# Inverses in 16-row blocks, a routing table by matrix products and a written-out order in a chunked recurrence with an expert layer

## The chip, the cores and the metric

The kernel runs on one core of a Trainium2 chip. The metric is device time in microseconds (us), the median of the runs shown. A core has the matrix engine TensorE (PE; its weight loads, PEld, overlap its products), VectorE (DVE), ScalarE (ACT), GpSimd (POOL) and the queues that issue transfers (SP above all here). Each engine takes its instructions in the order in which the program lists them. TensorE's clock is granted at one of two levels, 1.2 or 2.4 GHz; the profile prints 0.5 for the lower and 1.0 for the higher.

## The reference

Two parts, one after the other. The first is a recurrence over 768 steps for 4 batches and 8 heads with a 40x40 state:

```python
for t in range(S):
    y[:, :, t] = np.einsum('bhd,bhde->bhe', rt, state)
    Sa = np.einsum('bhde,bhe->bhd', state, at)
    state_decay = state * wt[:, :, None, :] - np.einsum('bhd,bhe->bhde', Sa, bt)
    state = state_decay + np.einsum('bhd,bhe->bhde', vt, kt)
```

Its output, as 3072 rows of 320, goes to a layer of 8 experts with one expert per row:

```python
expert_idx = np.argmax(x @ w_gate, axis=1)
...
if counts[e] < capacity:
    disp[e, counts[e]] = x[i]
...
h = np.maximum(np.einsum('ecd,edf->ecf', disp, w1), 0.0)
y = np.einsum('ecf,efd->ecd', h, w2)
...
out[i] = gate_w[i] * y[expert_idx[i], pos[i]]
```

## The kernel before, in words

**The scan.** The 768 steps are cut into 6 blocks (`i`) of 128, each of two chunks of 64 (`c`); batches go in two pairs (`pr`). For each block and pair `prep` loads w, a, k|b and r and multiplies them by running products of w (two scans of 1032 elements on VectorE). `unit` forms for each chunk the triangular 64x64 matrices of all 16 (batch, head): `nn` (evacuated to `ns`), `kk` (masked to `tm`) and the turned k|b (`bk`). `inverse` inverts the triangles of a whole block at once: the 32x32 diagonal blocks are transposed so that each partition holds one block (L562), are eliminated column by column in place (`elim`, L474 to L479), are transposed back (L486, L491), and `comb` joins the two 32-blocks of each 64 by two products. Block 0 alone (`SIX = (0,)`) eliminates 16x16 blocks and joins them first to 32 by products of 32 rows (`join`). `chain` then carries the state: `zz`, `sa` (a product with the inverse, written into `vu` beside v), `uT` (transposes of `vu`), `mT` (scores M, masked into `vu[:, 0]`), `yy` (outputs and new state in one accumulation, moving 128 columns per head), `turn` (the state turned). `gate` turns the outputs of a block to rows (x) and forms the logits with x as the stationary operand and `w_gate` moving. `route` picks the expert, counts places and scatters (expert slot, row, gate weight) to a table `meta` in DRAM, four indirect transfers per block.

**The experts.** For each expert the weights are loaded, scaled and split into two float16 parts (L1092, L1093), the rows of `meta` are loaded, turned to indices on POOL (L1126 to L1128), the rows of x are gathered by indirect transfers (L1131) and transposed by DMA (L1265), then come the products `hidden` (L1280), the ReLU and split (L1285, L1288), the products `result` (L1154) and the scatter of the output rows (L1160). Experts 0 and 1 take their first 384 rows from blocks 0 to 4 only, so they can begin before the last block is routed.

**The order.** Steps are put into named threads with their engines and buffers; a planner (`Schedule.order`) with costs, priorities (`LATER`) and choices between engines ("A...|V...") decides one order for all engines, and the program is emitted in it. PSUM has three double tiles `pp` and two single tiles `p1`; a step that takes one waits until its last reader is done.

## Time and profile before

| | us |
|---|---|
| runs shown | 667.86, 673.58, 674.64 |
| median | 673.58 |
| the profiled execution | 677.24 |
| its span (first to last instruction) | 675.5 |
| its mean granted clock | 0.874 |

The profiled execution is 3.7 us above the median. Its span leaves out 1.7 us before the first and after the last instruction. Busy times of an engine are unions of its instructions, so an engine that is busy 90% of a stretch may still be waiting in the other tenth for a result of another one. A product's record holds its way through the array; the distance from one start to the next tells what a stream costs.

### The profile page before, as it was taken

How to read it: one execution, taken by the hardware profiler on the slowest of the kernel's cores; microseconds unless marked ns; L12 is line 12 of the kernel's file. 1: busy time of each engine (PE TensorE's matmuls, PEld its weight loads, DVE VectorE, ACT ScalarE, POOL GpSimd, SP SyncE). 2: the span in 40 equal slices, each digit the busy share in tenths (PEclk: the TensorE clock that was granted, in tenths of full speed). 3: DMA queues.
4: the chain of work that ended last, by engine and by line, in shares of the span. 5: the costliest groups of instructions: out<-in, count | busy, mean ns of one | idle time of the engine just before them, and what ended most of it. 6: DMA issues, size and time to landing. Idle time of an engine off the chain costs nothing.

```text
span 675.5 us, 25339 instructions
## 1 busy us (share of the span) xinstructions
PE 551.9 (82%) x11268; PEld 428.6 (63%) x11268; DVE 437.5 (65%) x844; ACT 289.6 (43%) x567; POOL 154.7 (23%) x231
## 2 busy tenths in 40 slices
PE   1626989799588788899779789696997999999993
PEld 1525877688487678788768777553674455555462
DVE  6986788989896789799949825344443544545310
ACT  9513643644364245445623451233442545534320
POOL 6210010212023000310112022422243342352112
PEclk9665898999758696999879857967998999999998
DMA  6761044123502251235110231674739868957101
GB/s 177 202 168 35 4 113 142 59 78 108 147 30 21 73 143 48 57 80 150 45 34 15 61 113 33 115 209 125 208 87 207 232 158 255 245 125 199 38 11 43
DMA packets 71447, 74.19 MB, mean 110 GB/s; under 512 B 36399, under 2 KB 60177, under 8 KB 70368
## 3 DMA queue, kind: packets, MB, share of 16 engines
q1 hardware_dynamic: 67168, 62.79, 35.7%
q0 software_dynamic: 4160, 9.69, 4.9%
q8 instruction: 90, 1.47, 1.0%
q14 instruction: 29, 0.24, 0.1%
HBM read 57.17 MB, written 10.40 MB: 100 GB/s over the span
## 4 chain that ended last, share of the span: by engine, by line
issue 32%; PE 32%; DVE 17%; POOL 8%; DMA 4%; ACT 4%; SPq 1%; POOLq 1%; another core or an unknown queue 0%; DVEq 0%; ACTq 0%
PE pp L268 19%; PE p L268 7%; POOL out_dram L1160 4%; DVE tmp L477 4%; DVE nu L479 3%; PE pp L649 2%; POOL a L1131 2%; DMA px<-in_w_dram 2%; DVE vu L318 1%; DVE kb L371 1%; DVE xu L486 1%; POOL vT L1131 1%; DVE gx L351 1%; DVE px L360 1%; ACT ns L54 1%
## 5 line engine op out<-in xcount | busy, mean ns | idle before, releaser
L314 POOL TENSOR_SCALAR_AFFINE_SELECT tm<-tm 64x512 f32<-64x512 f32 x42 | 31.3, 746 | 163.7 <-ACT tm L312 148.6
L479 DVE TENSOR_TENSOR nu<-nu,tmp 128x87 f32<-128x87 f32 (+12 forms) x164 | 59.8, 365 | 5.6
L1160 POOL DMA_INDIRECT out_dram<-tm,ri x32 | 32.4, 1012 | 135.3 <-ACT tm L1315 104.0
L477 DVE TENSOR_TENSOR tmp<-xu,nu 128x87 f32<-128x87 f32 (+12 forms) x164 | 59.3, 361 | 4.2
L268 PE MATMUL pp<-vu,bk 128*40 128x128 f32 (+1 forms) x768 | 52.7, 295 | 6.3 <-DVE vu L318 4.7
L268 PEld LDWEIGHTS pp<-vu,bk 128*40 128x40 f32 x768 | 44.5, 129 | 11.4 <-DVE vu L318 5.4
L1280 PE MATMUL pp<-xT,kb 128*128 128x448 f16 (+5 forms) x256 | 47.2, 319 | 0.0
L268 PE MATMUL p<-nu,ns 64*32 64x32 f32 (+1 forms) x1024 | 23.6, 217 | 26.3 <-DVE nu L491 23.5
L50 POOL COPY x<-x 128x128 f16<-128x128 f16 x18 | 13.2, 734 | 137.6 <-ACT x L50 51.6
L268 PE MATMUL pp<-rv,vT 64*64 64x64 f32 x1536 | 34.0, 228 | 12.2 <-issue 8.3
L268 PE MATMUL pp<-a,kb 64*64 64x64 f32 x768 | 23.4, 274 | 22.8 <-DVE kb L371 20.4
L318 DVE TENSOR_TENSOR vu<-pp,mask 128x1024 f32<-128x1024 f32 x24 | 29.1, 1218 | 18.4 <-PE pp L268 16.8
L436 ACT ACTIVATE bk<-pp,sgn 128x320 f32<-128x320 f32 x48 | 22.6, 525 | 39.9 <-PE pp L268 26.5
L268 PEld LDWEIGHTS pp<-rv,vT 64*64 64x64 f32 x1536 | 28.8, 139 | 17.1 <-issue 11.5
L268 PEld LDWEIGHTS p<-nu,ns 64*32 64x32 f32 (+1 forms) x1024 | 21.8, 138 | 27.3 <-DVE nu L491 22.7
L1285 ACT ACTIVATE nt<-pp 128x448 f16<-128x448 f32 (+2 forms) x40 | 16.9, 476 | 48.9 <-PE pp L1280 43.7
L268 PE MATMUL p<-a,kb 64*64 64x64 f32 x768 | 32.6, 242 | 3.2 <-DVE nu L479 1.4
L268 PEld LDWEIGHTS pp<-a,kb 64*64 64x64 f32 x768 | 19.8, 180 | 24.2 <-issue 15.7
L1288 DVE SCALAR_TENSOR_TENSOR px<-pp,nt 128x448 f16<-128x448 f32 (+2 forms) x20 | 10.0, 539 | 38.2 <-ACT nt L1285 30.2
L1018 POOL DMA_INDIRECT meta<-mt,sloti x24 | 24.0, 1000 | 46.4 <-DVE mt L1015 33.4
L1280 PE MATMUL pp<-xT,px 128*128 128x448 f16 (+2 forms) x128 | 33.6, 322 | 0.2 <-DVE rv L1288 0.2
L268 PEld LDWEIGHTS p<-a,kb 64*64 64x64 f32 x768 | 29.9, 156 | 4.0 <-issue 1.5
(220 smaller groups left out, 1375.9 us busy)
## 6 DMA issues: line engine op xcount, KB each, us to landing
vu<-in_moe_w_dram SPq DMA_DIRECT2D x32, 320.0 KB
kb<-in_kb_dram SPq DMA_DIRECT2D x24, 320.0 KB
px<-in_w_dram SPq DMA_DIRECT2D x12, 512.0 KB
vu<-in_vt_dram SPq DMA_DIRECT2D x48, 128.0 KB
px<-in_moe_w_dram SPq DMA_DIRECT2D x12, 512.0 KB
xd<-x SPq DMA_DIRECT2D x24, 192.0 KB
a<-in_a_dram SPq DMA_DIRECT2D x24, 160.0 KB
rv<-in_rv_dram SPq DMA_DIRECT2D x24, 160.0 KB
```

The costliest lines, as they stand in the source:

```text
L268: TT.matmul(out, l, r, start=start, stop=True, skip_group_check=True)
L314: G.affine_select(out[half(x)], out[half(x)], pattern=[[0, n] for n in sh[1:-1]] + [[1, C]], compare_op=ALU.is_gt, fill=0.0, base=0, chann ...
L318: V.tensor_mul(out, in_, m.to_broadcast(sh))
L436: A.activation(U["bk"][:, x].rearrange("p h d -> p (h d)"), U["pi"][:, x, 0:HD], AF.Copy, scale=sgn[:, x:x + 1])
L477: V.tensor_mul(tv, xu[:, :, s + 1:ne, s:s + 1].to_broadcast([P, nb, n, m]), nu[:, :, s:s + 1, 0:m].to_broadcast([P, nb, n, m]))
L479: V.tensor_add(nu[:, :, s + 1:ne, 0:m], nu[:, :, s + 1:ne, 0:m], tv)
L649: TT.transpose(p[:, x, k * P:k * P + P], U["vu"][:, 1, x, k].rearrange("p r d -> p (r d)"), ident)
L1018: nc.gpsimd.indirect_dma_start(out=meta_v[t][:, :], out_offset=bass.IndirectOffsetOnAxis(ap=su[:, t:t + 1], axis=0), in_=mt[:, t, :], in_o ...
L1131: nc.gpsimd.indirect_dma_start(out=xt(j)[:c].rearrange("p a c -> p (a c)"), out_offset=None, in_=src[:, :], in_offset=bass.IndirectOffsetO ...
L1160: nc.gpsimd.indirect_dma_start(out=out_v[used[0] % (8 * E)][:, :], out_offset=bass.IndirectOffsetOnAxis(ap=ri.bitcast(U32)[:c, j, 1:2], ax ...
L1280: nc.tensor.matmul(s_["h", f + z][:, :n], l, rr, start=m % 7 == 0 and m < 14, stop=m >= 14)
L1285: nc.scalar.activation(s_["H"](0, f), s_["h", f][:, :n], AF.Relu)
```

## The change

- **Inverses.** All six blocks are eliminated as 16x16 blocks (14 steps with two blocks per partition instead of 30 steps). A step of 84 or more elements per partition is cut into two halves of rows, the second in a thread `inverse_b`. The join of 16 to 32 is done by products of 64 rows: `split` (two scaled copies with a mask of the 32-halves) lays the blocks out in `yq`, then 32 products into 64x32, `split` again, 32 products into 48x16, and a masked add on VectorE.
- **M and SA|v in one row.** `vu` holds M | SA|v | M in one row of 256, so `yy` moves 104 columns per head and not 128. v comes a second time, transposed, from DRAM (`load_x`, 24 transfers of 256 KB); `uT` transposes 64x64 blocks of SA alone, half as much to evacuate. The output of `yy` is taken in two instructions, not one.
- **Slot table by products.** Instead of `meta` in DRAM each block forms two one-hot matrices on VectorE (`hot_p`, 512 elements, `hot_j`, 3 x 192), multiplies them (4 products of 96 columns, `tabled`), and adds the result to a table in SBUF (`fold`); `index` turns the table to row indices and weights. The 24 scatters, the loads of `meta` and POOL's index instructions are gone.
- **Logits** with `w_gate` stationary: 8 products of 128 columns into four groups of 16 rows, a copy, and a product that adds the four groups.
- **139 unread products** (`warm`): float16, 128 stationary and 512 moving columns, written to the PSUM tile that the next step takes, before that step; nothing reads them. The list puts them in 88 places, all ahead of the last block's routing.
- **New order.** The planner is not used; the order is a list of step names in the text (`ORDER`), `/1` for the second choice of engine, `~n` for n unread products, and every load goes to SP.

```diff
+ORDER = """
+load_w load_kb decay0*2 decay_k0 inverse_0 load_a decay0 nn0*2 load_w load_kb decay1*2 unit decay_k1 load_v kk0
...
+    def warm(self, n, take):
+        for _ in range(n):
+            x = self.bufs[next(y for y in take if y in ("pp", "p1"))][0]
+            x = x if len(x.shape) == 2 else x[:, 0]
+            self.nc.tensor.matmul(x, self.spare[:, 0:P], self.spare[:, None, :].to_broadcast([P, 2, 2 * P]), start=True,
+                                  stop=True, skip_group_check=True)
...
-    SIX = (0,)
+    SIX = (0,1,2,3,4,5,)
...
+            rows = [(s + 1, ne)]
+            if nb * (ne - 1 - s) * m >= 84:
+                h = s + 1 + (ne - s) // 2
+                rows = [(s + 1, h), (h, ne)]
...
+        def split(y, x):
+            for z in range(2):
+                scale(two(y, z), x(z).rearrange("p (u x) t -> p u x t", x=2), mlo[:, z:z + 1])
...
         def join_a(pr):
             p = s_["p", pr] = get("p1")
             for u in range(16):
-                for q in range(4):
-                    mm(p[quarter(q), u * 16:u * 16 + 16], G_["ns"][quarter(q), pr * 16 + u, 0:32],
-                       s_["n1"][quarter(q), pr * 16 + u, 0:16], True)
+                for z in range(2):
+                    mm(p[half(z), u * 32:u * 32 + 32].rearrange("p (x t) -> p x t", x=2), G_["ns"][half(z), pr * 16 + u, :],
+                       s_["y", pr].rearrange("p (u x) (v t) -> p u x v t", x=2, t=16)[half(z), u // 2, :, u % 2], True)
...
         def take_jb(pr):
             x = s_["ntd"][:, pr * 16:pr * 16 + 16, 16:32]
-            V.tensor_add(x, s_["p", pr][:, 0:256].rearrange("p (u t) -> p u t", u=16), x)
+            V.scalar_tensor_tensor(x, s_["p", pr][:, 0:256].rearrange("p (u t) -> p u t", u=16), low[:, 0:1], x, ALU.mult,
+                                   ALU.add)
...
-                    TT.transpose(p[:, x, k * P:k * P + P], U["vu"][:, 1, x, k].rearrange("p r d -> p (r d)"), ident)
+                    y = half(1 - x)
+                    TT.transpose(p[:, x, k * C:k * C + C], U["vu"][y, x, k, C:3 * C], ident[y, y])
...
-            n = P if q < NQ - 1 else C
+            n = C + D if q < NQ - 1 else C
...
-            p = Q["pt"]
+            p = Q["pl"] = get("p1")
             for h in range(H):
-                mm(p[:, 0, R:R + 16], T["px"][:, h, 0:P], wge[:, h].rearrange("p x e -> p (x e)"), h == 0)
+                mm(p[32 * (h % 4):32 * (h % 4) + 16, 0:P], wge[:, h].rearrange("p x e -> p (x e)"), T["px"][:, h, 0:P], h < 4)
...
-        for bi in range(B):
-            add(lambda bi=bi, f=scatter: f(bi), "G1.04", gives=("route", i) if bi == B - 1 else None)
...
+            for bi in range(B):
+                TT.matmul(p[:, 0:NV], hp[:, bi * P:bi * P + P], hj[:, bi * NV:bi * NV + NV], start=bi == 0, stop=bi == B - 1)
...
+        def fold(ps):
+            nc.vector.tensor_add(tbl, tbl, ps[:, 0:2 * NJ].rearrange("p (v j) -> p v j", v=2))
```

**The order, at three places.** First VectorE in the middle of the elimination of block 1. Before (`xu` the transposed triangles, `nu` the inverse, `tmp` the product of a column and a row, `D` the state):

```order
L477 TENSOR_TENSOR tmp<-xu_118,nu_119 128x256
L479 TENSOR_TENSOR nu_119<-nu_119,tmp 128x16x16
L477 TENSOR_TENSOR tmp<-xu_118,nu_119 128x255
L479 TENSOR_TENSOR nu_119<-nu_119,tmp 128x15x17
L477 TENSOR_TENSOR tmp<-xu_118,nu_119 128x252
L479 TENSOR_TENSOR nu_119<-nu_119,tmp 128x14x18
L673 TENSOR_TENSOR D_146<-pp_94,g_0_149 104x8x40
```

and now:

```order
L633 TENSOR_TENSOR tmp<-xu_124,nu_125 128x70
L633 TENSOR_TENSOR tmp<-xu_124,nu_125 128x56
L638 TENSOR_TENSOR nu_125<-nu_125,tmp 128x2x5x7
L638 TENSOR_TENSOR nu_125<-nu_125,tmp 128x2x4x7
L633 TENSOR_TENSOR tmp<-xu_124,nu_125 128x64 x2
L638 TENSOR_TENSOR nu_125<-nu_125,tmp 128x2x4x8 x2
```

The row had each instruction read what the one before wrote; now two instructions that do not need each other stand side by side, each of a quarter of the elements. A block's elimination is 46 such instructions where it was 60.

Second TensorE where the inverses of block 1 are joined, in the change (`yq_131<-ns`: join_a, `xu,yq_131`: join_b, `nu,ns`: comb_a; `ident 128x512`: unread products; L829: uT; L574: the turned k|b; L961: the turned outputs). In the order before there are no joins here; comb_a follows the elimination at once.

```order
L403 MATMUL p_0_102<-yq_131,ns_123 64x32 x32
L403 MATMUL pp_101<-zs_141,nt_127 64x40 x16
L196 LDWEIGHTS ident
L196 MATMUL p_1_103<-ident 128x512
L196 LDWEIGHTS ident
L196 MATMUL p_1_103<-ident 128x512
L403 MATMUL p_1_103<-xu_124,yq_131 48x16 x32
L829 MATMUL pp_100<-ident,vu_139 128x64 x8
L574 MATMUL pp_101<-ident,kb_116 128x40 x16
L961 MATMUL pp_99<-ident,px_105 128x104 x8
L403 MATMUL p_0_102<-nu_125,ns_123 32x32 x32
```

Between the two products of a join stand `sa` of the other pair and two unread products; between the join and comb_a stand three steps of the chain.

Third POOL where the first expert rows are fetched. Before (`meta` the table in DRAM, `mm` its rows, `ri` the indices, `a` the gathered rows of x):

```order
L1018 DMA meta<-mt,sloti 6144x4 x8
L1126 TENSOR_SCALAR ri_209<-mm_206 128x3
L1127 TENSOR_SCALAR ri_209<-mm_206 128x3
L1128 TENSOR_SCALAR gs_213<-mm_206 128x3
L1131 DMA a_106<-xd,ri_209 128x768 x2
```

and now:

```order
L453 AFFINE_SELECT tm_119<-tm_119 64x512 x2
L1250 MEMSET acc 128x8 x2
L153 COPY x_0_148<-x_0_148 128x2x64 x2
L1384 DMA a_112<-xd,ri_7416 128x768
L1384 DMA vT_142<-xd,ri_7416 128x768
```

The scatters and the index instructions are gone from POOL; the gathers read indices that VectorE wrote.

Other counts of the two programs: masks by a copy on ACT and two selects on POOL, 21 before and 7 now, the other 17 now one instruction each on VectorE (3 before); evacuations of `nn` (three instructions each) all 24 on ACT before, 11 on VectorE now; `zs` on VectorE 8 times (1 before).

## Rows read from the trace of the kernel before

**Rows 1.** The profile's page: busy time, share of the span and instructions of two engines, and TensorE's granted clock in 40 slices of the span, in tenths.

```profile
PE 551.9 (82%) x11268; PEld 428.6 (63%) x11268; DVE 437.5 (65%) x844; ACT 289.6 (43%) x567; POOL 154.7 (23%) x231
PEclk9665898999758696999879857967998999999998
```

**Rows 2.** Busy time by stretch: the stretch and its length, then the busy us (instructions) of PE, PEld, DVE, ACT and POOL, the granted clock, the share of the DMA engines and GB/s. The first four make up the span: start, the five periods from one block's elimination to the next, the last block, the experts. The fifth is one of the five periods.

```profile
0.00:31.00 31.00, 10.64 (x256) 10.22 (x256) 24.96 (x26) 22.81 (x33) 13.07 (x48) 0.83 0.76 205
31.00:345.40 314.40, 248.63 (x7544) 224.27 (x7542) 262.44 (x517) 142.04 (x295) 49.74 (x64) 0.84 0.30 81
345.40:455.00 109.60, 93.25 (x2116) 79.26 (x2113) 61.84 (x169) 36.87 (x82) 25.11 (x37) 0.80 0.36 89
455.00:675.50 220.50, 199.38 (x1366) 114.82 (x1364) 88.22 (x136) 87.90 (x159) 66.77 (x82) 0.96 0.56 148
144.90:204.70 59.80, 48.38 (x1362) 44.18 (x1361) 54.78 (x115) 28.41 (x62) 9.45 (x11) 0.80 0.31 95
```

**Rows 3.** The same view for the four longest stretches at the lower clock before the experts.

```profile
37.60:71.70 34.10, 18.34 (x867) 17.40 (x868) 24.88 (x43) 9.46 (x17) 0.00 (x0) 0.50 0.35 86
177.60:201.40 23.80, 15.49 (x445) 14.83 (x447) 22.84 (x46) 12.53 (x24) 3.75 (x4) 0.50 0.17 52
382.40:402.80 20.40, 15.99 (x388) 14.96 (x388) 10.03 (x37) 10.50 (x18) 3.79 (x7) 0.50 0.29 94
437.00:450.60 13.60, 10.31 (x44) 7.73 (x44) 4.89 (x29) 1.81 (x7) 2.16 (x4) 0.50 0.82 222
```

**Rows 4.** The two elimination lines by stretch (length, DVE busy, count, clock, DMA): L477, then L479, each for block 0 (16x16) and block 1 (32x32).

```profile
31.00:76.40 45.40, 4.40 (x14) 0.62 0.31 77
76.40:144.90 68.50, 10.63 (x30) 0.95 0.30 85
...
31.00:76.40 45.40, 4.51 (x14) 0.62 0.31 77
76.40:144.90 68.50, 11.27 (x30) 0.95 0.30 85
```

**Rows 5.** VectorE instruction by instruction (start, us), and two groups by shape (busy, mean ns of one, idle before). The first two need each other; the two of the third row do not.

```profile
38.54 0.29 DVE L477 TENSOR_TENSOR tmp<-xu,nu 128x128 f32<-128x128 f32 x1
38.86 0.29 DVE L479 TENSOR_TENSOR nu<-nu,tmp 128x128 f32<-128x128 f32 x1
45.12 1.30 DVE L491 STREAM_TRANSPOSE nu<-xu 128x512 f32<-128x512 f32 x2
...
L491 DVE STREAM_TRANSPOSE nu<-xu 128x512 f32<-128x512 f32 x4 | 2.7, 701 | 0.1
L479 DVE TENSOR_TENSOR nu<-nu,tmp 128x60 f32<-128x60 f32 x10 | 2.2, 222 | 0.3
```

**Rows 6.** The joins of block 0, in order of time: join_a of the first pair, then its correction and its last transpose on VectorE, and the last transpose of the second pair.

```profile
45.89 1.90 PE L268 MATMUL p<-nu,ns 32*32 32x16 f32 x128 [11.23 <-DVE nu L491]
...
51.97 0.42 DVE L518 TENSOR_TENSOR xu<-p,xu 128x256 f32<-128x256 f32 x1 [3.30 <-issue]
52.43 0.71 DVE L491 STREAM_TRANSPOSE nu<-xu 128x512 f32<-128x512 f32 x1
...
63.62 0.71 DVE L491 STREAM_TRANSPOSE nu<-xu 128x512 f32<-128x512 f32 x1
```

**Rows 7.** Steps of TensorE in order of time (start, us): comb_a at the lower clock; a stretch at the higher clock with yy, the turned k|b, uT, zz; the logits; comb_a at the higher clock.

```profile
64.48 1.92 PE L268 MATMUL p<-nu,ns 64*32 64x32 f32 x64 [1.44 <-DVE nu L491]
...
81.53 1.95 PE L268 MATMUL pp<-vu,bk 128*40 128x128 f32 x32
83.41 0.69 PE L428 MATMUL pp<-ident,kb 40*128 40x40 f32 x16
...
84.51 1.09 PE L649 MATMUL pp<-ident,vu 128*128 128x128 f32 x8
85.53 0.68 PE L268 MATMUL pp<-vu,tm 64*64 64x40 f32 x32
86.01 0.66 PE L268 MATMUL pp<-D,a 64*64 64x40 f32 x32
...
106.89 1.96 PE L268 MATMUL pp<-wge,px 128*128 128x16 f32 x16
...
120.48 1.20 PE L268 MATMUL p<-nu,ns 64*32 64x32 f32 x64
```

**Rows 8.** Six float16 products of 320 columns in a row, at the lower and at the higher clock.

```profile
467.70 1.81 PE L1154 MATMUL p<-ns,vT 128*128 128x320 f16 x6
...
475.27 0.99 PE L1154 MATMUL p<-ns,vT 128*128 128x320 f16 x6
```

**Rows 9.** Work that changes its engine: a mask and an evacuation, where they stand now (first: VectorE in order of time; then ACT and POOL by shape).

```profile
73.68 0.67 DVE L318 TENSOR_TENSOR tm<-p,mask 128x512 f32<-128x512 f32 x1
...
L54 ACT ACTIVATE ns<-pp 32x256 f32<-32x256 f32 x48 | 18.0, 375 | 1.0
L54 ACT ACTIVATE ns<-pp,neg 128x512 f32<-128x512 f32 x24 | 16.5, 687 | 20.4 <-PE pp L268 14.8 <-remote 5.3
```

**Rows 10.** The last table's way through DRAM, on POOL: the last scatter, the first index instruction and its wait, the gather.

```profile
452.46 0.98 POOL L1018 DMA_INDIRECT meta<-mt,sloti  x1 [0.30 <-issue]
459.56 1.26 POOL L1126 TENSOR_SCALAR ri<-mm 128x1 int32<-128x1 f32 x1 [6.12 <-DMA mm<-meta]
...
461.47 1.15 POOL L1131 DMA_INDIRECT a<-xd,ri  x1 [0.17 <-POOL gs L1128]
```

More of the change, by code (lines that the diff above doesn't have):

```diff
@@ L84, in emit, with listed @@
             fn = threads[name][at[name]][0]
+            self.warm(new.get("warm", 0), threads[name][at[name]][4])
             fn()
             at[name] += 1
+    def warm(self, n, take):
[4 more added lines that the diff above has]
+                                  stop=True, skip_group_check=True)
+    def listed(self):
+        at, order = dict.fromkeys(self.threads, 0), []
+        for x in self.given.split():
+            x, n = (x.split("*") + [1])[:2]
+            x, warm = (x.split("~") + [0])[:2]
+            name, m = (x.split("/") + [0])[:2]
+            for _ in range(int(n)):
+                ops = self.threads[name][at[name]][1]
+                ops = ops[int(m)] if ops else []
+                que = ["S" for par in ops for e, d in par if e == "L"]
+                order.append((name, que or ([int(m), ops[0][0][0]] if ops else []), {"warm": int(warm)}, 0.0, {}))
+                at[name] += 1
+        assert all(at[x] == len(y) for x, y in self.threads.items()), "not every step is listed"
+        return order
     def order(self, mu):
@@ L265, in half, with at, skew @@
         return slice(C * x, C * x + n)
+    def at(r, o=0):
+        return slice(o + (C + O) * r, o + (C + O) * r + D)
+    def skew(x, lo, *dims):
+        f = flat(x)
+        return AP(tensor=f.tensor, offset=f[:, lo:].offset, ap=[f.ap[0]] + [list(y) for y in dims])
     def mm(out, l, r, start):
@@ L322, in prep, with loads @@
         n = (pr, i)
-        def loads(kind, src, rows):
+        def loads(kind, src, rows, lo=0):
             def go():
@@ L566, in inverse @@
         add(begin2, "V1.97", needs=[("nn", (pr, 2 * i + c)) for pr in range(2) for c in range(2)] + [("unit", i)], take=["xu"])
-        for s in range(ne - 1):
-            add(lambda s=s: elim(s), f"V{(nb * (ne - 1 - s) * (s + 1) + 160) / 960 * 2:.3f}")
+        add(first, "V.2", gives=("row", i, 0, 0))
+        both = False
+        for s in range(1, ne - 1):
+            parts = elim(s)
+            for x, (mul, fold, cost) in enumerate(parts):
+                more = add if x == 0 else steps("inverse_b")
+                more(mul, cost, needs=[("row", i, s - 1, 0)] * x)
+                more(fold, cost, needs=[("row", i, s - 1, 1 - x)] * both, gives=("row", i, s, x))
+            both = len(parts) == 2
         if nb == 1:
@@ L755, in chain @@
         more = steps(f"uT{pr}")
-        more(uT, "P1.0", needs=[("vu", n)], take=["pp"])
-        more(take_uT, "A1.0|V1.22", take=["vT"], free=["pp"], gives=("uT", n))
+        more(uT, "P.6", needs=[("vu", n)], take=["pp"])
+        more(take_uT, "A.56|V.62", needs=[("load_x", n)], free=["pp"], gives=("uT", n))
         if q:
@@ L820, in gate @@
         add = steps(f"gat{late(i)}{pr}")
-        add(turn_y, "P1.0", needs=[("y", (pr, 2 * i)), ("y", (pr, 2 * i + 1))], take=["pp"])
-        add(logits, "P1.6", needs=[("wge", 0)], free=["px"])
-        add(take_logits, "A.2|V.2", gives=("logits", n))
+        done = [("y", (pr, 2 * i)), ("y", (pr, 2 * i + 1))]
+        add(turn_y, "P1.0", needs=done, take=["pp"], gives=("turn_y", n))
+        more = steps(f"logi{late(i)}{pr}")
+        more(logits, "P.5", needs=done + [("wge", 0)], take=["p1"])
+        more(parts, "A.25|V.25", needs=[("turn_y", n)])
+        more(fold, "P.25", free=["px"])
+        more(take_logits, "A.2|V.2", free=["p1"], gives=("logits", n))
         add(x_hi, "A.46 A.46|V.49 V.49", take=["x16"])
@@ L855, in scan_part @@
         L_ = {}
-        first, count, place, gates, scatter = route(i, L_)
-        add(first, "V1.9", needs=[("logits", (pr, i)) for pr in range(2)] + [("gated", i - 1) if i else ("fill", 0)],
+        first, count, place, gates, hot_p, hot_j, fold, index = route(i, L_)
+        add(first, "V1.9", needs=[("logits", (pr, i)) for pr in range(2)] + [("gated", i - 1)] * (i > 0),
             gives=("one_hot", i))
@@ L872, in scan_part @@
     PLAN[0] = GT
-    steps("fill")(lambda: fill(dma), "G.5 L0>.4&L0>.55&L0>.55&L0>.55&L0>.55", needs=[("nt", 0, 0)], gives=("fill", 0))
     def m4(x, n=1):
@@ L1059, in route_all @@
+        whole = i == NI - 1 or EARLY and i == NI - 2
+        return (first, count, place, lambda: gate(glob, s_["d"], B, tiles), hot_p, hot_j, fold, index if whole else None)
+    route.columns = 2 * NJ
     def route_all(pool, ps):
@@ L1344, in expert @@
                 add(lambda j=j, o=o, c=c, part=part: result_(j, o, c, part), "P.8" if c == P else "P.42", take=["p1"] * (part == 0),
-                    needs=([("l", key, part * 2 + z) for z in range(2)]
-                           + [("w", wkey, 3 + part)] * (wkey is not None)) if j == chunks[0][0] else (),
+                    needs=([("l", key, part * 2 + z) for z in range(2)] * (j == chunks[0][0])
+                           + [("w", wkey, 3 + part)] * (wkey is not None and j == chunks[0][0])
+                           + list(before) * end),
                     free=(["hh"] * 4 + ["W"] * 6 * last) * end,
```

372 lines of the change are left out of this document (278 added, 94 removed).

## The prediction

> **What bounds the kernel now.** I read the totals and the clock first, then the busy times by stretch, then the single instructions of the stretch that matters. Over the span TensorE is busy 82% and VectorE 65% [rows 1], which hides two different programs. From 455 us on TensorE is busy 199.4 of 220.5 us at a clock of 0.96 [rows 2]: the experts run at the speed of their products, and the change leaves these alone. In the 314.4 us of the five periods VectorE is busy 262.4 us (83.5%) and TensorE 248.6 us (79%) at a mean clock of 0.84; in the best period VectorE reaches 54.78 of 59.80, or 91.6% [rows 2]. Neither is a clean bound: VectorE fills most, and TensorE, which it waits for, falls to the lower clock wherever it has gone slack. In four long stretches at that clock TensorE does 60.1 us of work [rows 3], and a step that takes 1.20 us at the higher clock takes 1.92 at the lower [rows 7], so a full clock would do that work in about 0.6 of the time.
>
> I make the sum by stretches against the profiled execution (677.2 us, span 675.5), which is 3.7 us above the median.
>
> **VectorE in the five periods.** The elimination of a 32x32 block costs 10.63 + 11.27 = 21.9 us, that of block 0 with 16x16 costs 4.40 + 4.51 = 8.9 [rows 4]. Four blocks in this stretch change over: 4 x 13.0 = 52 us off, and some 4 us of the 0.03 us that lie between two instructions that need each other (0.29 long, 0.32 apart [rows 5]). Cutting a step in halves I cost at nothing: two of 128 elements take 2 x 0.32 = 0.64 us, four of 60 take 0.22 each [rows 5] and, being independent, can start 0.07 to 0.10 early, as the two transposes do (1.30 together, 2 x 0.70 singly [rows 5]): 4 x 0.15 = 0.60. A rule speaks against this. The Trainium skill ("VectorE: DVE Perf Modes", section Terms) says that a pipeline flush follows every instruction and that the next cannot issue until the pipe is empty. By it four quarters would take 4 x (0.22 + 0.03) = 1.00 us, 0.36 more than now in each of 9 steps; the trace does not agree, since the two transposes take 0.10 less together than singly.
>
> What comes on: transposes of half a block, four of 0.70 where there was one of about 1.24 by that size, and two corrections of 0.42 [rows 5, 6], 4 x 2.4 = 10 us; the work moved from ACT and POOL, a mask 0.67 and an evacuation 0.69 + 2 x 0.38 by its ACT rows [rows 9], 14 x 0.67 + 11 x 1.45 and 7 copies of `zs` of some 0.45, five sixths of it here, 24 us; the output taken in two, about 3; the one-hots and the table, about 2.3 us per block by size from the same rows, 9. Half of the evacuations of `uT` fall away, 1. Sum: 262.4 - 56 + 45 = 251 us. So VectorE's own total hardly shrinks; the elimination, a chain of 60 dependent instructions, is exchanged for work that can go anywhere. At the old fill 251 us need 301 us, at the best fill of rows 2 they need 274. I take 90%, 279 us, near the better end, since TensorE comes faster and the elimination no longer stands in the way of the chain. **Gain 35 us, bounds 13 and 40**; with no idle at all 251, gain 63.
>
> **TensorE in the same stretch** must fit into 279 us. `uT` costs 1.02 from its start to the next step [rows 7]; a quarter of each transpose and half the evacuation is left, between 0.25 and 1.02, I take 0.5: 20 x 0.5 = 10 us off. `yy` costs 1.88 for 128 columns [rows 7], 1.53 for 104: 7 us off. The logits cost 1.96 [rows 7]; 8 products of 128 columns by the rate of `yy` (16 in 1.88, two at a time) take 0.94, or half of that four at a time, plus the folding product: I take 0.8, 9 x 1.1 = 10 off. The joins cost like comb_a, 1.1 us each at the higher clock: 20 x 1.1 = 22 on, less four of 1.9 in block 0 [rows 6], so 14 on. The table products, four of 96 columns in float32, about 1.2 us per block, 5 on. The clock: 33.8 us of work in the two long stretches here at 0.6 of the time, 13 off [rows 3]. The unread products: six of 320 columns start 0.138 us apart at the higher and 0.27 at the lower clock [rows 8], so 512 columns cost 0.22 to 0.43, and some 115 of the 139 fall here: 25 us on, 50 at the lower clock. Sum 248.6 + 4 = 253 us, 90% of 279. That fits only if the unread products fall into gaps; without them TensorE is 82% full.
>
> **The last block, 345 to 455.** The elimination is 13 us shorter where VectorE is 83% full or more until it ends: 10 off. TensorE works 16.0 + 10.3 us at the lower clock [rows 3]; 0.4 of it is 10 us, I count half. The table's way: the last scatter ends at 453.4, the gather starts at 461.5 [rows 10]; instead come the one-hots, the product and the indices, some 5 us from the same start (the first scatter is 4 us before the last), so the gather could start 8 us sooner, but TensorE is idle only some 6 us in that time. 4 off, 3 of them behind 455. Against it the table, the moved work and the joins, 4 on. **Gain 16 us, bounds 5 and 28.**
>
> **The rest.** The start changes nothing: its chain is loads and scans. The experts' products are the same, hidden behind nothing. **Gain 3 us, bounds 0 and 6.** The second copy of v, 24 x 256 KB, and the loads that now all go through SP's queue lie where the DMA engines are 30% busy [rows 2]; I cost them at nothing, and it would cost a wait per chunk if they came late.
>
> Sum: 677.2 - 35 - 16 - 3 = 623 us in the terms of the profiled execution, 620 in those of the median. With all bounds: 655 down to 599.
>
> **Rivals.**
> - *Deeper (0.22).* The new order fills VectorE to 95% (264 us, 50 off), the last block gains 25 and the transition 6: 677 - 81 - 4 = 592. For it: 91.6% is reached already under a planner with coarser costs. Against it: two engines at 95% at once are nowhere in rows 2.
> - *The unread products cost what they return (0.15).* They stand in TensorE's queue in 88 places; where the step behind them was ready, each delays it by 0.22 or 0.43. Each place also changes the shape of the tiles twice: between equal shapes a step starts 0.20 us before the last one's record ends, between different ones 0.07 [rows 7], so 176 changes cost 0.13 each, 23 us. If that comes on top of 253, TensorE is the bound at 276 us and with 95% needs 290: gain 24, not 35, and the last block gains 8: 642; if the clock stays as it is in spite of them (the change not doing what it says), 13 more in the periods: 655. I take 646. The Trainium skill ("TensorEngine Tiling (Array Packing)", Key Properties) states that a change of the tiling mode drains the engine; the trace shows a drain of that small size only.
> - *Halves do not overlap (0.03).* By the flush rule above 0.36 x 9 x 6 = 19 us more of VectorE, at 90% 22 us: 642.
> - *The joins stay exposed: slower (0.05).* In block 0 the inverse of the first pair is ready 7.3 us after join_a began and that of the second 18.4 [rows 6]; a 32x32 block has no such wait. The join goes VectorE, ACT, TensorE, ACT, TensorE, VectorE, and each step queues in order behind the chain of the other pair. If 15 us of it stand open in five blocks, that is 75 us, all that the elimination gives (5 x 15 with its gaps), and the 45 us that VectorE takes on are then unpaid: about 677 - 75 + 75 + 30 - 7 = 705, 700 by the median. It decides from about 10 us open per block. Against it: in block 0 nothing else was there to fill the wait, and TensorE ran at the lower clock.
> - *Nothing to be told from no change (0.05):* fill falls back to 80% as the fixed list meets other durations: about 668 to 680.
>
> **Numbers.** The forecast of 620, with 604 to 637 as its own range, has 0.50. The deeper case adds the low end, the unread products the high end: 590 to 650 holds the forecast, half of the deeper case and nearly all of the two at 642 to 646, 0.79. A difference within 1% (667 to 680) cannot be told from none here. Faster 0.90, same 0.05, slower 0.05.
>
> **What would show it.** From one big transpose of `ns` to that of the next block five times: 279 us in all, 55.8 on average (62.9 now). VectorE busy about 251 us in it. The elimination lines near 9 us per block, with halves starting before their neighbours end. The granted clock in the scan at 0.95 or more. `uT` near 0.5, yy near 1.5, logits under 1 us. The gather of the last rows no longer behind a DRAM wait. I am wrong if VectorE waits for TensorE between the two halves of a join, if TensorE's clock still falls for 20 us at a time, or if TensorE's idle time moves to the front of the experts.

## The result and the profile after

| | before | after |
|---|---|---|
| runs shown, us | 667.86 to 674.64 (4) | 639.54 to 643.97 (4) |
| median, us | 673.46 | 641.38 |
| ratio, 95% interval | | 0.954 [0.948, 0.961] |
| the profiled execution, its span | 677.24, 675.5 | 641.26, 639.5 |

The kernel is 32 us faster, where 53.5 were forecast. From the page after: busy times and TensorE's clock in 40 slices, which answer to [rows 1], then the chain that ended last, by engine, and below it the same line of the page before. This chain is followed back from the last instruction to what released it, step by step; "issue" is time in which the engine waited for nothing that the profile shows.

```profile
PE 589.2 (92%) x12503; PEld 445.4 (70%) x12503; DVE 424.1 (66%) x958; ACT 271.1 (42%) x562; POOL 102.7 (16%) x146
PEclk9765997989779986998599996899989999999999
PE 61%; issue 21%; POOL 6%; DMA 1%; ACT 1%; POOLq 1%; DVE 0%; SPq 0%; another core or an unknown queue 0%; ACTq 0%
...
issue 32%; PE 32%; DVE 17%; POOL 8%; DMA 4%; ACT 4%; SPq 1%; POOLq 1%; another core or an unknown queue 0%; DVEq 0%; ACTq 0%
```

VectorE had 17% of the chain and has nothing of it now; TensorE holds 61% where it held 32%. In the five periods alone the chain by line is:

```profile
by line: PE pp L403 35.1%; PE p L403 30.3%; PE pp L196 5.8%; PE p L196 5.0%; issue 4.4%; PE pp L574 3.4%; PE pp L961 2.9%; PE p L866 2.2%; PE pp L829 2.1%; PE p L1065 0.6%; ACT yq L157 0.6%; ACT nt L153 0.4%; PE p L1259 0.2%; PE p L1258 0.2
```

TensorE's lines add up to 88% there, the unread products (L196) to 11%. The clock still falls in a slice or two of every period. Busy time by stretch (columns as in [rows 2]): the five periods, then the last block up to the first product `hidden`, from there to the end, and the first 34 us of that.

```profile
27.85:338.52 310.67, 293.60 (x8420) 244.91 (x8420) 246.16 (x574) 126.73 (x290) 15.67 (x27) 0.84 0.36 100
338.52:422.10 83.58, 78.79 (x2417) 69.04 (x2414) 58.04 (x177) 33.71 (x77) 6.37 (x10) 0.90 0.43 112
422.10:639.50 217.40, 205.16 (x1450) 122.65 (x1450) 96.57 (x181) 90.10 (x167) 67.06 (x63) 0.99 0.60 159
422.10:456.00 33.90, 33.90 (x239) 20.75 (x240) 23.77 (x70) 16.56 (x33) 6.52 (x9) 1.00 0.71 200
```

The same stretches of before, cut at the first `hidden` too (the periods are in [rows 2]):

```profile
345.40:436.20 90.80, 77.74 (x2042) 68.81 (x2038) 55.08 (x136) 31.89 (x69) 19.98 (x31) 0.83 0.27 64
436.20:675.50 239.30, 214.89 (x1442) 125.27 (x1438) 94.97 (x168) 92.89 (x171) 71.90 (x88) 0.94 0.58 153
436.20:470.00 33.80, 24.64 (x125) 15.35 (x122) 16.05 (x45) 11.58 (x23) 7.94 (x10) 0.71 0.60 159
```

So the 36 us between the two spans are: start 3 (31.0 to 27.9), five periods 4 (314.4 to 310.7), last block 7, experts 22. Of these 22, TensorE is idle 12 us less (24.4 to 12.2) and busy 10 us less (214.9 to 205.2, at a clock of 0.99 and not 0.94). The periods, from which 35 were to come, gave almost nothing: VectorE has 16 us less to do there, but TensorE went from 248.6 us of 314.4 to 293.6 of 310.7, at the same clock of 0.84. The groups of TensorE in the periods (busy, mean ns of one record, idle before): join_a, the unread products in two, join_b, yy, uT, and the logits in two.

```profile
L403 PE MATMUL p<-yq,ns 64*64 64x32 f32 x640 | 27.4, 249 | 7.0 <-ACT yq L157 4.2 <-issue 2.7
L196 PE MATMUL pp<-ident 128*128 128x512 f16 x69 | 24.2, 411 | 0.0
L403 PE MATMUL p<-xu,yq 64*48 64x16 f32 x640 | 22.0, 216 | 0.8 <-ACT yq L157 0.4 <-issue 0.3
L196 PE MATMUL p<-ident 128*128 128x512 f16 x55 | 20.4, 436 | 0.0
...
L403 PE MATMUL pp<-vu,bk 128*40 128x104 f32 x522 | 29.6, 270 | 0.0
L829 PE MATMUL pp<-ident,vu 64*128 64x64 f32 x136 | 8.3, 245 | 0.0
L403 PE MATMUL p<-px,wge 128*16 128x128 f32 x128 | 6.3, 326 | 0.0
L403 PE MATMUL p<-pick,px 128*128 128x16 f32 x16 | 3.6, 300 | 0.0
```

The records overlap; from each start to the next start, idle time left out, the joins come to 47 us and the unread products to 38. A float32 product leaves two records, so the 32 products of a join_a are 64 records; an unread float16 product leaves one. The price of a join is best read where the steps stand side by side at the lower clock (TensorE in order of time): join_a, comb_a, join_b, then `nn`, comb_a, `kk`. Below them stand a join_b at the higher clock, and `kk` in the kernel before at the higher clock.

```profile
50.84 3.62 PE L403 MATMUL p<-yq,ns 64*64 64x32 f32 x64
54.39 1.92 PE L403 MATMUL p<-nu,ns 32*32 32x32 f32 x64
56.24 2.75 PE L403 MATMUL p<-xu,yq 64*48 64x16 f32 x64
...
61.63 1.11 PE L403 MATMUL pp<-a,kb 64*64 64x64 f32 x32
62.67 1.92 PE L403 MATMUL p<-nu,ns 32*32 32x32 f32 x64
64.52 1.97 PE L403 MATMUL p<-a,kb 64*64 64x64 f32 x32
...
99.26 1.61 PE L403 MATMUL p<-xu,yq 64*48 64x16 f32 x64
...
80.45 1.15 PE L268 MATMUL p<-a,kb 64*64 64x64 f32 x32 [1.37 <-DVE nu L479]
```

Sixty-four records take 3.62, 2.75 and 1.92 us for 64, 48 and 32 stationary columns, whatever moves (32, 16 and 32 columns). `nn` and `kk` have one shape, but `nn` goes round four tiles of the array and `kk`, like the joins, only two: 1.11 against 1.97.

Much of the joins runs where the clock is low, 579 of their 1280 records. Two stretches of the periods at the lower clock, which answer to [rows 3]; in them lie the joins of block 0 and the end of those of block 4:

```profile
39.75:67.05 27.30, 24.13 (x585) 22.87 (x587) 23.21 (x31) 9.96 (x20) 0.00 (x0) 0.50 0.22 61
299.17:319.64 20.47, 19.76 (x343) 16.95 (x343) 8.09 (x20) 4.31 (x10) 0.58 (x2) 0.50 0.31 96
```

In the second one TensorE is busy 19.76 of 20.47 us, so the lower clock does not stand only where TensorE has gone slack, as the prediction had it.

VectorE did what was forecast. Two quarters take 0.25 from one pair to the next:

```profile
31.47 0.33 DVE L638 TENSOR_TENSOR nu<-nu,tmp 128x48 f32<-128x48 f32 x2
31.72 0.34 DVE L633 TENSOR_TENSOR tmp<-xu,nu 128x60 f32<-128x60 f32 x2
31.97 0.34 DVE L638 TENSOR_TENSOR nu<-nu,tmp 128x60 f32<-128x60 f32 x2
```

The gathers stood behind loads of the table from DRAM [rows 10] and now wait for VectorE's indices. The first of them starts at 407.92 (424.48 before), the first that needs the last block's routing at 446.34 (461.47 before). The last two rows are the slots of the last block, after and before, from which the way to that gather starts.

```profile
407.92 1.27 POOL L1384 DMA_INDIRECT a<-xd,ri  x1 [26.62 <-DVE gs L1302]
446.34 1.04 POOL L1384 DMA_INDIRECT vT<-xd,ri  x1 [10.73 <-DVE ri L1301]
...
438.17 0.17 DVE L1271 CAST sloti<-slot 128x4 int32<-128x4 f32 x1
...
447.55 0.17 DVE L1052 CAST sloti<-slot 128x4 int32<-128x4 f32 x1
```

That way takes 8.2 us where it took 13.9.

### The profile page after: what moved, and what is told of

It reads as the page before. It is cut to its first block, busy times and chain, and to the rows that moved or that the text cites. A ratio compares the mean times of both kernels' runs of the same rounds, so it can differ in the third digit from the quotient of the medians.

```text
span 639.5 us, 27724 instructions
## 1 busy us (share of the span) xinstructions
PE 589.2 (92%) x12503; PEld 445.4 (70%) x12503; DVE 424.1 (66%) x958; ACT 271.1 (42%) x562; POOL 102.7 (16%) x146
## 4 chain that ended last, share of the span: by engine, by line
PE 61%; issue 21%; POOL 6%; DMA 1%; ACT 1%; POOLq 1%; DVE 0%; SPq 0%; another core or an unknown queue 0%; ACTq 0%
PE pp L403 24%; PE p L403 18%; PE pp L1538 3%; POOL out_dram L1413 3%; PE pp L196 3%; PE p L196 3%; POOL a L1384 2%; PE pp L574 2%; PE pp L961 2%; PE p L866 2%; PE p L1407 2%; PE pp L829 2%; PE p L1065 1%; DMA xT<-a 1%; DMA vu<-in_moe_w_dram 1%
## 5 line engine op out<-in xcount | busy, mean ns | idle before, releaser
L403 PE MATMUL pp<-vu,bk 128*40 128x104 f32 (+1 forms) x768 | 43.2, 272 | 0.0
L453 POOL TENSOR_SCALAR_AFFINE_SELECT tm<-tm 64x512 f32<-64x512 f32 x14 | 12.4, 887 | 162.1 <-ACT tm L450 161.6
L403 PE MATMUL p<-yq,ns 64*64 64x32 f32 x768 | 31.5, 244 | 7.0 <-ACT yq L157 4.2
L403 PEld LDWEIGHTS p<-yq,ns 64*64 64x64 f32 x768 | 30.0, 164 | 8.5 <-issue 7.8
L403 PE MATMUL pp<-a,kb 64*64 64x64 f32 x768 | 19.7, 251 | 16.6 <-DVE px L489 13.9
L1538 PE MATMUL pp<-xT,ns 128*128 128x448 f16 (+2 forms) x192 | 34.2, 313 | 0.0
L1384 POOL DMA_INDIRECT a<-xd,ri x25 | 28.3, 1134 | 36.3 <-DVE gs L1302 26.6
L153 ACT COPY vu<-pp 64x320 f32<-64x320 f32 x42 | 17.6, 420 | 35.6 <-PE pp L403 30.7
L490 DVE TENSOR_TENSOR_SCAN gx<-px,z 104x1032 f32<-104x1032 f32 x12 | 27.7, 2308 | 3.1 <-DMA px<-in_w_dram 2.8
L510 DVE TENSOR_TENSOR kb<-kb,gx 104x1024 f32<-104x1024 f32 x24 | 29.8, 1281 | 0.0
L1546 DVE SCALAR_TENSOR_TENSOR px<-pp,rv 128x448 f16<-128x448 f32 (+1 forms) x32 | 18.6, 602 | 16.5 <-ACT rv L1543 15.0
```

The costliest lines, as they stand in the source:

```text
L153: (e.copy if e is self.nc.scalar else e.tensor_copy)(out, in_)
L403: TT.matmul(out, l, r, start=start, stop=True, skip_group_check=True)
L490: V.tensor_tensor_scan(T["gx"][0:R, 0:H * (P + 1)][:, ::-1], T["px"][0:R].rearrange("p h t -> p (h t)")[:, ::-1], z2[0:R].rearrange("p h t ...
L510: V.tensor_mul(x, x, g[:, :, None, half(c)].to_broadcast([R, H, 2, C]))
L1384: nc.gpsimd.indirect_dma_start(out=xt(j)[:c].rearrange("p a c -> p (a c)"), out_offset=None, in_=src[:, :], in_offset=bass.IndirectOffsetO ...
L1538: nc.tensor.matmul(s_["h", f + z][:, :n], l, rr, start=m % 7 == 0 and m < 14, stop=m >= 14)
```

## The experiments

The kernel before ran beside every batch of runs. Its median differed between batches (651 to 674 us, both on one chip, for a reason that no run shows), so ratios to it are given; between batches they are good to some 1.5% only, as the next run shows. The question is why the periods did not get shorter.

**The changed kernel again**, as the measure for the rest.

> The changed kernel once more, as the measure for the runs beside it. 0.948 to 0.961 of the kernel before on the same chip, if the gain does not hang on the chip.

637.8 us, before 655.6: 0.9685 [0.961, 0.976]. The changed kernel's own time is nearly that of the first comparison (641.4); the gain is 3% here and was 4.6% there because the kernel before was faster in this batch. The runs with twice the unread products, with join_a twice and with 16x16 blocks alone ran in the same batch.

**Without unread products, and with twice as many.**

```diff
-load_a decay1 nn0~1 kk0 kk0~2 kk0/1 load_x nn0/1 nn1~1 load_w nn1 nn1~2 decay0 nn1 inverse*3
+load_a decay1 nn0 kk0 kk0 kk0/1 load_x nn0/1 nn1 load_w nn1 nn1 decay0 nn1 inverse*3
...
```

> The changed kernel without its 139 unread products; everything else and the list of steps as it is. Theory A (they cost what they return): in the five periods of the changed kernel TensorE is busy 293.6 of 310.7 us, 38.1 of it in unread products, and its clock stands at the lower level for 106 us as before the change, so they did not hold it. Without them TensorE has 255 us to do there and VectorE 246: the periods take 280 to 295 us, 612 to 628 in all. Theory B (they do hold the clock in the other 205 us): without them the lower level spreads, every 10 us of work that falls to it takes 7 us more, and the time is 640 to 665, above all in the first two periods.

632.2 us (615.3 to 644.0), before 657.2: 0.962, too scattered for an interval, and in another batch than the changed kernel: the two are not told apart.

> The changed kernel with 278 unread products, two for each one. Theory A (each costs what it takes): 139 more of 0.27 to 0.52 us, so 35 to 45 us slower than the changed kernel. Theory B (they hold the clock): the 106 us at the lower level in the five periods shrink to under 60, which gives back some 20 of it: 10 to 25 slower. Theory C (TensorE would wait for its instructions in that time: the gaps without a releaser stand every 128 products and end 1.4 to 1.6 us after 16 KB have landed on its instruction queue; 26.6 us of such gaps without unread products, 10.5 with them): the first 139 replaced 16 us of such waits, the second 139 find at most 10 left: 28 to 40 slower.

653.9 us, before 655.6: 0.995 [0.990, 1.000], 16 us behind the changed kernel. The five periods of the three kernels, columns as in [rows 2]: none, 139 (the repeat of the changed kernel), 278.

```profile
28.60:338.60 310.00, 271.36 (x8296) 246.34 (x8294) 245.05 (x576) 126.04 (x290) 16.67 (x27) 0.80 0.37 100
```
```profile
29.70:343.90 314.20, 293.92 (x8412) 245.17 (x8412) 246.60 (x576) 126.16 (x289) 17.61 (x27) 0.84 0.37 99
```
```profile
28.40:350.20 321.80, 299.00 (x8521) 237.59 (x8520) 247.42 (x575) 125.90 (x288) 16.72 (x27) 0.92 0.35 96
```

The clock follows the dose (0.80, 0.84, 0.92), so the unread products do hold it: theory B is right in its mechanism, and for the doubled ones in its size too (10 to 25 us slower forecast, 16 measured). But the periods are 310, 314 and 322 us (311 in the first profile of the changed kernel). Counted from start to start, TensorE's other work in them falls from 273 to 256 and 238 us, while the unread products take 0, 37 and 61. What they give back in clock they take themselves; without them TensorE also idles 39 us instead of 20. The first 139 about pay for themselves, within what these runs can tell; the next 139 do not pay. The forecasts of 280 to 295 us in the periods (theory A) and of 640 us or more in all (theory B) for the run without them both fail.

**Joins of 32 rows**, alone and without unread products.

```diff
         def join_a(pr):
...
-                for z in range(2):
-                    mm(p[half(z), u * 32:u * 32 + 32].rearrange("p (x t) -> p x t", x=2), G_["ns"][half(z), pr * 16 + u, :],
-                       s_["y", pr].rearrange("p (u x) (v t) -> p u x v t", x=2, t=16)[half(z), u // 2, :, u % 2], True)
+                for q in range(4):
+                    mm(p[quarter(q), u * 16:u * 16 + 16], G_["ns"][quarter(q), pr * 16 + u, 0:32],
+                       s_["n1"][quarter(q), pr * 16 + u, 0:16], True)
```

> The changed kernel with the joins done as block 0 did them before: 64 products of 32 rows instead of 32 of 64 rows for each step, one plain copy instead of four scaled copies for each pair. Theory A (the joins are mis-sized TensorE work on the bounding engine): a 64-row join_a takes 3.62 us at the lower and 2.05 at the higher clock, join_b 2.74 and 1.5, where the 32-row joins took 1.9 to 2.0 each at the lower one; 4 to 5 of the 10 pairs of the periods join at the lower level, so TensorE has 8 to 14 us less to do and the time falls to 626 to 634. Theory B (the joins lie under VectorE's work and TensorE's excess is only filled time): 637 to 643, no change.

671.9 us (658 to 674), before 657.2: 1.024 [1.018, 1.031], against 0.9685 some 5 to 6% slower than the changed kernel, where both theories had it faster or equal.

> Both edits, no unread products and joins of 32 rows. Theory A: TensorE has 243 us left in the five periods, less than VectorE's 246, so the second edit gives less than alone: 605 to 622. Theory B: 640 to 665, as without the unread products alone.

666.6 us: 1.012 [1.005, 1.018]; outside both as well, and 34 us above the run without unread products in the same batch. In the periods of the first of the two kernels TensorE does 10 us less work than in the changed kernel, and yet they last 326 us:

```profile
28.20:354.60 326.40, 283.83 (x9692) 234.75 (x9691) 245.15 (x572) 114.72 (x264) 17.12 (x27) 0.81 0.35 95
```

The time went into waits with no releaser ("issue"). TensorE in order of time, with the idle time before in brackets; below it what it waited for in the periods (us, times, longest), and the DMA queues between 57.2 and 58.5 us.

```profile
42.24 1.90 PE L403 MATMUL p<-nu,ns 32*32 32x16 f32 x128 [2.49 <-DVE nu L653]
44.07 0.61 PE L196 MATMUL p<-ident 128*128 128x512 f16 x1
44.72 1.90 PE L403 MATMUL p<-xu,yq 32*32 32x16 f32 x126
48.10 0.28 PE L403 MATMUL p<-xu,yq 32*32 32x16 f32 x2 [1.49 <-issue]
...
59.95 1.35 PE L403 MATMUL p<-xu,yq 32*32 32x16 f32 x82 [5.85 <-issue]
```
```profile
PE p L403 <- issue: 29.6, 17, 5.8
PE pp L403 <- issue: 8.4, 5, 5.8
```
```profile
q1 hardware_dynamic: 69, 0.23, 55.0%
q8 instruction: 1, 0.02, 5.4%
```

The step of 128 records stops after 126 of them, in the middle of a row of equal products. Counting TensorE's records from the start of the program, the waits that end at 48.1, 51.6, 59.9 and 63.4 us come after 604, 732, 860 and 988 records: 128 apart. Each ends 1.2 to 1.6 us after 16,384 bytes have landed on the queue q8 (so do 21 of the 24 gaps above 0.3 us in the periods, 33.3 us in all); the landing shown in the last fence is over at 58.38, and the wait ends at 59.95. Landings on that queue never start less than 3.1 us apart in any run (3.2 in this one and before, 3.4 after). The Trainium skill ("Runtime: NRT & Kernel Launch", Instruction fetch mechanics) says that an engine's instructions come in blocks of 16 KiB, 256 instructions each, through its own DMA queue, and that crossing from one block to the next is mostly hidden. The trace agrees on the block (128 records with their 128 weight loads); that it is hidden does not hold here. The same count gives some 10 us of such waits in the periods before the change, 10.5 after, 19 without unread products, 33 with joins of 32 rows, 50 with both edits. So the 64-row products do not save array time (47 us, where the 32-row ones take 36); they halve the instructions of the joins. The unread products are long work for few instructions, which would let the next block arrive; the 19 us without them and 10.5 with them fit that.

**join_a twice**, the second time over the same result.

```diff
-            for u in range(16):
+            for u in [*range(16), *range(16)]:
```

> The changed kernel with the 32 products of each join_a issued twice, the second time over the same result, so that nothing else changes: 2.05 us (higher clock) to 3.62 (lower) more for each of 12 pairs, 768 more records, six blocks of instructions. Theory A (TensorE is the bound of the periods, and what the joins take shows in the time): 24 to 36 us slower. Theory B (VectorE or a chain of waits is the bound): under 10 slower.

669.2 us: 1.020 [1.010, 1.030], 31 us slower than the changed kernel in the same batch: theory A.

```profile
28.50:367.20 338.70, 317.45 (x9052) 270.02 (x9052) 246.05 (x576) 126.05 (x289) 16.85 (x27) 0.84 0.34 92
```

Against the repeat of the changed kernel TensorE has 23.5 us more in the periods and they are 24.5 longer, while VectorE has the same 246. Work of the joins shows in full. By itself this could also be a chain of waits through the joins, which the edit lengthens too; but TensorE is idle only 17 of the 311 us of the changed kernel, and it holds 88% of the chain there and VectorE nothing. TensorE is the bound.

**One part alone, and all parts without the written order.**

```diff
-    SIX = (0,)
+    SIX = (0, 1, 2, 3, 4, 5)
```

> The kernel before with one part of the change: all six blocks eliminated as 16x16, joined by products of 32 rows as block 0 was, in the planner's order. Theory A (VectorE is the bound, and 13 us less of elimination in five blocks count in full): 30 to 55 us faster than the kernel before. Theory B (the joins stand open in this order: in block 0 the two pairs were ready 7.3 and 18.4 us after join_a began): between 10 faster and 40 slower.

759.2 us: 1.152 [1.141, 1.164].

```diff
-        self.later, self.given = later, given
+        self.later, self.given = later, None
```

> The changed kernel's steps in the order that the planner gives them, as before the change, instead of the written list; so no unread products either, and loads spread over two queues by its rule. Tells what the written order is worth. Theory A (the new parts bring the gain, the order little): within 10 us of the run without unread products. Theory B (the parts only move work from the elimination to TensorE and the order brings the gain): 655 to 690, close to the kernel before.

737.9 us: 1.122 [1.115, 1.130]. Both are far beyond the worst case expected. The periods of the two, columns as in [rows 2]:

```profile
31.60:390.10 358.50, 279.74 (x9301) 255.25 (x9297) 213.68 (x403) 141.31 (x304) 33.87 (x41) 0.75 0.26 71
```
```profile
30.10:395.70 365.60, 280.69 (x8118) 254.92 (x8120) 236.36 (x540) 147.39 (x341) 23.29 (x37) 0.74 0.31 85
```

What VectorE waited for at the correction of the joins (us, times, longest): in the kernel before with 16x16 alone, in the planner's order of all parts, in the changed kernel.

```profile
DVE xu L518 <- PE p L268: 43.4, 8, 9.5
```
```profile
DVE xu L688 <- PE p L403: 80.7, 10, 11.4
```
```profile
DVE xu L688 <- PE p L403: 14.9, 8, 4.8
```

The same steps leave 80.7 us open in the planner's order and 14.9 in the written one. That is not all that the planner's order costs: the granted clock is 0.75 and 0.74 in these periods (0.84 before, 0.80 in the written order without unread products), and in the first of the two TensorE waits 32 us for instructions, as with joins of 32 rows above. Against the run without unread products the planner's order of all parts is 56 us longer in the periods and 49 behind them; the second half was not followed up. In the planner's order the short elimination costs time; in the written order, with the other parts, it gains (without it 0.999, below).

**The inverses undone, the rest kept**, with the 60 elimination steps of a block spread over the places of the 46 in the list.

```diff
-    SIX = (0,1,2,3,4,5,)
+    SIX = ()
...
-            if nb * (ne - 1 - s) * m >= 84:
+            if nb == 2 and nb * (ne - 1 - s) * m >= 84:
```

> The changed kernel with one part undone: all blocks eliminated as 32x32 as five were before (60 instructions, no halves), no joins, the elimination's instructions spread over the same places of the list; 132 unread products, since seven stood at join steps. TensorE has the joins' 47 us less to do in the five periods and 1280 records less to fetch (10 blocks of 128), VectorE 52 us more of elimination and about 14 less of transposes, corrections and scaled copies: 284 for 246. Theory A (TensorE's work bounds the periods, so the joins cost more than the short elimination gives): 290 to 305 us in the periods, 615 to 632 in all, 0.94 to 0.965 of the kernel before. Theory B (VectorE becomes the bound): at 90% of its time 315 us, 640 to 650, 0.975 to 0.99. Theory C (the next block waits for its late inverse): 20 to 40 us more than B, over 1.0.

674.6 us: 0.999 [0.994, 1.004].

> As the run beside it, without any unread products. If they only fill time in which TensorE waits (now for VectorE), the time is the same within 1.5%. If they keep up the clock for a chain that waits in turn for TensorE, it is 2 to 5% slower than with them; if they cost what they take, 2 to 5% faster.

674.0 us: 0.997 [0.992, 1.003]: the same with and without unread products. The periods of the first:

```profile
28.30:364.50 336.20, 253.45 (x7125) 204.89 (x7125) 296.41 (x616) 110.96 (x254) 16.95 (x27) 0.82 0.33 92
```

VectorE is busy 296 of 336 us (88%): the mechanism of theory B, with 12 us more work than I had counted. Its time is C's, so the 336 cannot be split between the two with certainty; the list was stretched by hand. In this order, with 32x32 inverses, the periods are 22 us longer than before the change (314), and what lies behind them is 21 shorter (309 for 330 us), so the other parts return there what the periods lose. With 16x16 VectorE falls to 246 us and TensorE takes over.

**Unread products only around the joins.** First: doubled from 25 steps ahead of a block's first join to its last comb, none elsewhere. Second: as they are in that stretch, and two more ahead of each join product step, one ahead of each comb product step.

```diff
-load_a decay1 nn0~1 kk0 kk0~2 kk0/1 load_x nn0/1 nn1~1 load_w nn1 nn1~2 decay0 nn1 inverse*3
...
-inverse*2 inverse_b kk1~3 kk1/1 iden1~1 iden1 kk1 inverse_b inverse*9 kk1 zz1~2 load_kb decay0 decay_k0 join0
+inverse inverse_b inverse inverse inverse_b kk1~6 kk1/1 iden1~2 iden1 kk1 inverse_b inverse inverse inverse inverse
...
```

> The changed kernel with its unread products doubled where they stand from 25 steps ahead of the first join of a block to its last comb step, and left out everywhere else: 156 in all. In every block the clock falls to the lower level there, in the joins (from 39.7, 125, 169, 234 and 299 us on), and with twice as many everywhere that lower time went from 105 us to 58. Theory A (where they stand matters): lower time of 50 to 70 us with hardly more of them than now, 5 to 15 us faster than the changed kernel on the same chip (0.945 to 0.96 of the kernel before). Theory B (only their number counts): as the changed kernel or up to 8 us slower (0.968 to 0.98).

636.7 us, before 651.3: 0.977 [0.970, 0.985].

> Unread products kept from 25 steps ahead of the first join of a block to its last comb step, left out elsewhere, and two more ahead of every join product step, one more ahead of every comb product step: 150 in all. As the run beside it, with the products inside the joins rather than around them. Theory A: 0.945 to 0.96 of the kernel before. Theory B: 0.968 to 0.98. If they delay the joins themselves, each pair waits 1.2 to 2 us longer, 12 to 24 us in all: 0.98 to 1.0.

638.1 us (630.5 to 646.8): 0.980 by the medians. Both lie at the edge of theory B in time, and in time they are no better than the changed kernel (637.8 us and 0.9685, in another batch). In the clock theory A is right: it is 0.92 in the periods with 156 of them, as with 278 in all places. The periods of the first:

```profile
28.80:332.00 303.20, 277.56 (x8443) 231.00 (x8443) 246.33 (x575) 126.12 (x289) 16.73 (x27) 0.92 0.39 104
```

In this execution, the fastest of its four, the periods are 11 us shorter than in the repeat of the changed kernel and 7 shorter than in its first profile; in the second run's profile they are 304 us. The medians do not bear a gain out, and the changed kernel did not run beside them, so it stays open. No version here beats the changed kernel beyond doubt.

## Why the prediction was right and wrong

The sign and the range were right; 641 stands next to the rival at 642 to 655, in which TensorE becomes the bound, and not at 620. That it stands inside the range is partly luck: the periods gave 4 us where 35 were forecast, and what made up for it came from elsewhere, 10 us more than forecast behind them and 3 at the start. Without these the time would be some 654.

- **VectorE, 262 to 251 us:** 246.2. The elimination takes 9.0 per block (9 forecast). Halves start before their neighbours end, 0.50 for four quarters where I counted 0.60, so the rival of halves that do not overlap falls.
- **The fill of 90%:** failed; 79%. In the run with 32x32 inverses, where VectorE has most to do, it reaches 88%. Here it was not the bound, as the chain and the doubled join_a show. This is the step that broke the 35 us: a fill read while VectorE led was carried over to a program in which another engine leads.
- **TensorE, 248.6 + 4 = 253 us:** 293.6. `yy` fell by 7 (7 forecast), `uT` by 13 (10), the logits by 8 (10); the table takes 2 (5). The joins are mis-sized: "like comb_a, 1.1 us each at the higher clock" made 22 us, and they take 47. They have 64 and 48 stationary columns where comb_a has 32; at the higher clock a join_a takes 2.0 us and a join_b 1.5, which would make 35, and the other 12 come from the lower clock. `kk`, with the same 64x64 tiles, was in the trace before and would have given the price (1.15 us for 32 records at the higher clock, so some 2.3 for 64); that the number of tiles in turn makes it, I read from `nn` and `kk` and did not try by itself. The unread products take 38 and not 25: 21 of the 124 ran at the lower clock, where I had counted all at the higher, and before a step of another shape one takes 0.30 us at the higher clock, not 0.22.
- **The clock, 13 us off:** failed; 0.84 in the periods before and after, and from 39.7 us it still falls for 27 us at a time. The unread products do lift it (0.80 without them), but much of the added joins runs while it is low. That it falls wherever TensorE has gone slack does not hold either: from 299 us it is low with TensorE busy 97% of the time.
- **What they cost:** the rival's price of 23 us for changes of tile shape is not what made it true, though some 7 us of it stand behind the unread products; it was 25 us more of joins, 13 more of unread products and the 13 that the clock did not return.
- **The last block, 16 us, and the rest, 3:** 7 and 22. The parts are cut elsewhere, at the first `hidden`; the sum is 29 for 19. The 16 was a slip: its terms, 10 + 5 + 4 - 4, make 15 at most. The table's way was to be 8 us shorter and is 5.7 (8.2 for 13.9); I allowed 4 us for it, because TensorE "is idle only some 6 us in that time". But in the first 34 us of the experts it was idle 9 and at a clock of 0.71; now it is busy throughout at 1.00, and idles 12 us to the end instead of 24. The gather waits for no load from DRAM any more. Which part gives the 22 is argued and not shown: no run takes out the table alone. The run with 32x32 inverses has nearly all of it, so it does not come from the inverses.
- **The joins stay exposed, slower (0.05):** in the written order 14.9 us, not 75. But the planner's order of the same parts leaves 80.7 us open and is 12% slower than the kernel before. The mechanism was right, and the written order prevents most of it. The price of 75 us open was met; the time of 705 that it led to was not (738 us, with a lower clock and 49 us behind the periods), and it was summed wrongly besides: 677 - 75 + 75 + 30 - 7 is 700.
- **Missed altogether:** TensorE waits for its instructions, some 10 us of the periods before the change, among the waits without a releaser. It stood in no term.

## What to carry to other kernels

When the bounding engine is relieved, size the new work of the next engine from rows of the same tile shape, and do not carry over a fill that was read while the other engine led. Where TensorE stops in the middle of a row of equal products, count the records between the stops: stops 128 apart were waits for instructions here, and fewer, larger products help though the array works no less. Parts that trade a long chain on one engine for short steps across several are worth what the order hides of their waits; try the parts and the order apart.

## What the runs showed of the hardware that was not expected

- Blocks of 128 records of small products run dry: waits of up to 5.85 us, each ended by a 16 KB landing, with landings begun no closer than 3.1 us. A block of 128 records at the 19 ns of comb_a (1.20 for 64 [rows 7]) would last 2.4 us by this estimate, less than those 3.1. Before the longest wait the landing began at 57.3 us, 8.1 after the one before; the DMA engines were 65% busy from 54.2 to 59.9 us, but that the loads made it late was not tried.
- The clock is worth something to a program of small products, and unread products cost what it is worth: doubling them took the clock in the periods from 0.84 to 0.92 and TensorE's other work from 256 to 238 us, and the periods grew by 8 us. Confining them to the joins gave 0.92 with hardly more of them, and no gain that the medians show.
- At the lower clock each of 64 records in two tiles costs 30, 43 and 57 ns for 32, 48 and 64 stationary columns (32, 16 and 32 columns moving; 32 stationary columns cost the same with 64 rows [rows 7] as with 32).
